# The last steps before the experts: weights 44 and 45 fetched ahead, unread products on TensorE, and a softmax step moved on VectorE

## The chip, the cores and the metric

The kernel runs on one core of one Trainium2 chip. Its time is the device time of one execution in microseconds (us). [...]

## The reference

Attention with a memory term, and after it a soft mixture of experts over the attention's output:

```python
scores = scale * np.matmul(q, k.transpose(0, 1, 3, 2))          # 8 batches, 8 heads, 576 rows, 64 wide, causal
a = softmax(scores); local = a @ v
mem_out = (phi(q) @ M_prev) / (phi(q) @ z_prev)                 # phi = elu + 1
x = g * mem_out + (1 - g) * local                               # reshaped to 4608 x 512
logits = x @ phi                                                # 32 slots
d = softmax of logits over the 4608 rows
slot_input = d.T @ x                                            # 8 experts, 4 slots each
slot_out[e] = relu(slot_input[e] @ w1[e]) @ w2[e]               # w1 512x1024, w2 1024x512
c = softmax of logits over the 32 slots
out = c @ slot_out                                              # 4608 x 512
```

All data are 32-bit floats. The softmax over the 4608 rows must be complete before the first expert can start, so attention and experts can't overlap.

## The kernel before

**Two halves.** The list `SEQ` writes the attention out by hand, 32 head pairs, with the logits and the running softmax over rows between them. Each word is an operation, the head pair or row group it works on (`y` for the one-off steps at the end), and after a colon the PSUM slot that it takes (0 to 3, two banks each). Every engine takes its instructions in the order in which the words emit them; the function `pin` fixes it. Behind the list come the experts, written as plain calls: `f1` (first layer, four of them), `f2` (second layer), `g1` and `g2` (sum over experts), and 18 times `comb`, which makes one block of the output (512 KB) and stores it.

**Weights.** They are 64 blocks of 512 KB. Block x goes where `WORD[x]` says: an empty word is a tile of its own, a name is a buffer of the attention that is no longer used (`FREE`). The words `w@0` to `w@43` fetch 44 blocks during the attention. The other 20 are fetched by the loop over `reload` behind `f1(1,1)` in the program, into the tiles of blocks 0 to 19, each as soon as its `f1` has read the old block. All these transfers and all stores are issued by SyncE (SP) in order. `STAGE` names the block tiles in which `comb` puts its results.

**The chain between the halves.** For the last head pair `mu@31` (VectorE, L485) scales the attention, `ad.0@31` adds its two parts into `x` (L502; the table `EV` says on which engine). `x3.3@7` transposes them on TensorE (L429), `x3e.3` copies them out (ScalarE), `x1.3` multiplies with phi (L610), `y4` takes the running minimum (VectorE, L620). `y6`, `y6m`, `y8` and `y8n` bring the minimum over all slots to `ngm`; `y5` makes the exponentials, `y7` and `y7e` transpose them; `y9.0` and `y9.1` (L742) sum the last rows of x with them into one PSUM tile, `y9a.0` and `y9a.1` (L747) add that tile's halves to `acc`; `y8e` makes `es` (L734); `y10` (L756) gives the experts' input, `y10e` copies it out, and `f1(0,0)` (L847) can start. `y11` and `y12` (L766) are for the denominator.

**The other softmax.** `z1` transposes the logits of eight row groups (TensorE, L429) into PSUM slot 0, and `z2` takes from them, in four VectorE instructions (L786, L787), the minimum over each row's slots. `c0` reads the result, behind `f1(0,0)` on ScalarE.

The last words of the list, with the chain in them, and how a product's tile is taken:

```python
ad.1@31 m.0@31 w@40:+ x1.0@7:2 dn.0@31 x1.1@7 x1.2@7 mu.0@31 w@36:+ ad.0@31 x3.3@7:0 w@41:+ x3e.3@7 x1.3@7 y4@y w@42:+
y6@y:2 y5@y z1@y:0 y6m@y y7@y:3 y8@y w@43:+ z2@y y7e@y y9.0@y:3 y9.1@y y8n@y y9a.0@y y8a@y y9a.1@y y8e@y y11@y y10@y:3
y12@y y10e@y y12e@y
```

Of the kernel before, what the change touches and what calls it, by code (L numbers as in the profile page):

```python
# [176 lines left out]
mx.2.0@31 m.1@30 ex.2.1@31 yz@y t.A@31:1 dn.1@30 ex.2.0@31 w@34:+ x3.1@7:2 mu.1@30 ex.0.1@31 t.B@31:3 te.AX@31  # L177
te.AY@31 ad.1@30 x3e.1@7 av.1@30:0 te.BX@31 w@35:+ te.BY@31 av.0@30 ex.1.0@31 m.0@30 t.C@31:3 dn.0@30 w@37:+ mu.0@30
av.2@31:2 te.CY@31 te.CX@31 ad.0@30 av.3@31 w@38:+ m.1@31 x3.2@7:3 w@39:+ dn.1@31 av.1@31:0 mu.1@31 x3e.2@7 av.0@31
ad.1@31 m.0@31 w@40:+ x1.0@7:2 dn.0@31 x1.1@7 x1.2@7 mu.0@31 w@36:+ ad.0@31 x3.3@7:0 w@41:+ x3e.3@7 x1.3@7 y4@y w@42:+  # L180
y6@y:2 y5@y z1@y:0 y6m@y y7@y:3 y8@y w@43:+ z2@y y7e@y y9.0@y:3 y9.1@y y8n@y y9a.0@y y8a@y y9a.1@y y8e@y y11@y y10@y:3
y12@y y10e@y y12e@y
""".split()

EV = {o: e for e, x in dict(
    a="""
# [17 lines left out]
    p="""  # L204
# [21 lines left out]
        ate@10 te.CY@16 te.CX@16 x2a@3 te.AY@19 te.BX@19 ate@12 te.CY@20 x3e.0@5 te.AY@22 te.CY@22 x3e.2@5 te.CX@23  # L226
        te.AY@25 x3e.0@8 te.BX@25 te.CX@25 te.AY@26 te.BX@26 x3e.1@6 te.CY@26 te.CX@27 te.BX@29 te.BX@30 te.CX@30
        te.AY@31 te.BX@31
    """,
).items() for o in x.split()}  # L230

GO = [0, 1, 2, 3, 4, 5, 8, 6, 7]
WORD = ['', '', '', '', '', '', '', '', '', '', '', '', '', '', '', '', '', '', '', '', '', '', 'xa0', 'xa1', 'au', 'qk0', 'K', 'X', 'p3', 'p2', 'p1', 'qk1', 'x0', 'x1', 'K', 'X', 'xd0', 'p3', 'p2', 'p1', 'at0', 'at1', 'vm', 'xd1']
WARM = 6
STAGE = [20, 21, 22, 23, 24, 25, 26, 27, 28, 29, 30, 31, 32, 33, 34, 35, 36, 37]


@with_exitstack
def tile_attn_soft_moe(ctx, tc, qk, vm, au, beta, phi, w1, w2, cst, out):
    nc = tc.nc  # L240
# [3 lines left out]
    cs = const.tile([128, 256], F32, name="cs")  # L244
    ident = cs[:, 0:128]
# [446 lines left out]
    def op_w(x):  # L692
        wload(x, *(FREE[WORD[x]] if WORD[x] else (wres, f"w{x}", None)))

    y = {}

    def op_y4(_):
        slot_max(cT[:, 8], xs[GO[8]]["p1"][:, 0:128], mrun[0], mrun[1])  # L700
# [141 lines left out]

    def f1(eg, f):
        ps = pf()
        for c in range(4):
            for g in range(4):
                nc.tensor.matmul(ps[32 * g:32 * g + 32, :], si[:, c, 32 * (4 * eg + g):32 * (4 * eg + g) + 32],  # L847
                                 wt[0, eg, f, c // 2, g][:, c % 2, :], start=c == 0, stop=c == 3)
        h = hs[eg, f] = dbl.tile([128, 512], F32, name="f")
        nc.scalar.activation(h, ps, AF.Relu)  # L850

# [63 lines left out]
    def comb(dh, g):  # L915
# [110 lines left out]
```

## Time and profile before

| | us |
|---|---|
| median of 3 runs | 412.38 |
| lowest and highest run | 409.0 and 412.43 |
| the profiled execution | 411.43 |
| its span, first to last instruction | 409.7 |
| attention, up to the last head pair's sums | to about 337 |
| chain between the halves | 337.4 to 347.5 |
| experts, until the last block is computed | 347.5 to 398 |
| last stores, nothing else running | 398 to 408 |

Times below are microseconds from the start of the span. 1.7 us of the execution lie outside the span.

### The profile page before, as it was taken

What the parts mean: (1) busy time and instruction counts of PE and PEld (TensorE: products, weight loads), DVE (VectorE), ACT (ScalarE), POOL (GpSimd) and SP (SyncE); (2) the same over time, 40 slices, a digit from 0 to 9 for tenths busy, and PEclk for the clock granted to TensorE, in tenths of its full rate; (3) what the DMA queues carried; (4) which work ended last, traced back from release to release, by engine and by line L of the source; (5) the groups of instructions that cost most, each with busy time, mean ns of one, the idle gap of its engine ahead of it and who ended that gap; (6) DMA issues with size and microseconds to landing.
All of it is one profiled execution on the core that took longest, in us unless ns stands there. A gap on an engine that the chain in (4) does not pass through costs nothing.

```text
span 409.7 us, 19301 instructions
## 1 busy us (share of the span) xinstructions
PE 371.6 (91%) x8115; PEld 301.3 (74%) x8115; DVE 303.2 (74%) x1136; ACT 295.6 (72%) x741; POOL 198.0 (48%) x255
## 2 busy tenths in 40 slices
PE   7799999989899999999989999999999977999970
PEld 3688987878788878888979788888897864244350
DVE  2879888889888898889888798888988645232560
ACT  1778998788889788989878779877898721211560
POOL 0647765477648637666657476654765310000000
PEclk9889999999999999999999999999999996899995
DMA  8425554745556564666656533434537985599998
GB/s 280 128 83 156 180 173 146 243 133 192 162 164 190 188 211 120 195 193 182 179 150 195 159 102 97 126 117 137 197 102 223 341 301 203 230 407 390 333 334 261
DMA packets 35542, 80.97 MB, mean 198 GB/s; under 512 B 3328, under 2 KB 12800, under 8 KB 35456
## 3 DMA queue, kind: packets, MB, share of 16 engines
q1 hardware_dynamic: 35168, 79.66, 60.3%
q8 instruction: 64, 1.05, 1.1%
q14 instruction: 22, 0.18, 0.2%
q10 hardware_dynamic: 288, 0.08, 0.1%
HBM read 70.29 MB, written 9.44 MB: 195 GB/s over the span
## 4 chain that ended last, share of the span: by engine, by line
PE 49%; ACT 24%; DVE 16%; issue 4%; DMA 3%; SPq 1%; POOLq 0%; POOL 0%; DVEq 0%; ACTq 0%
ACT p L426 13%; PE psD L461 11%; PE psD L429 9%; PE psD L393 9%; DVE p L420 7%; ACT at L290 6%; PE pf L847 4%; PE pf L864 4%; PE psD L471 4%; DVE at L293 3%; DMA qk<-in_qk_dram 2%; ACT xd L290 2%; PE pa L921 2%; DVE w L485 1%; PE psD L654 1%
## 5 line engine op out<-in xcount | busy, mean ns | idle before, releaser
L426 ACT ACTIVATE p<-p,nm 128x576 f32<-128x576 f32 (+3 forms) x256 | 144.1, 608 | 12.4 <-DVE nm L420 11.9
L420 DVE CUSTOM_DVE_ANT_0 p<-psD,mk 128x448 f32<-128x448 f32 (+3 forms) x256 | 127.4, 536 | 9.3 <-PE psD L393 7.0
L461 PE MATMUL psD<-vm,at 128*64 128x65 f32 x2560 | 89.8, 224 | 4.7 <-DVE at L293 2.0
L393 PE MATMUL psD<-K,X 64*128 64x320 f32 (+3 forms) x768 | 91.8, 355 | 2.0 <-DVE at L293 0.5
L290 ACT COPY at<-psD 128x512 f32<-128x512 f32 (+1 forms) x153 | 77.7, 551 | 20.3 <-PE psD L429 17.8
L461 PEld LDWEIGHTS psD<-vm,at 128*64 128x64 f32 x2560 | 80.8, 138 | 14.0 <-issue 3.2
L429 PE MATMUL psD<-cs,p 64*128 64x64 f32 x1408 | 65.4, 227 | 7.4 <-ACT p L426 4.4
L393 PEld LDWEIGHTS psD<-K,X 64*128 64x128 f32 x768 | 63.5, 188 | 8.4 <-DVE at L293 1.0
L429 PEld LDWEIGHTS psD<-cs,p 64*128 64x128 f32 x1408 | 57.6, 140 | 13.1 <-ACT p L426 6.6
L502 POOL TENSOR_TENSOR x<-w 128x256 f32<-128x256 f32 x64 | 46.9, 734 | 36.1 <-DVE w L485 35.1
L485 DVE TENSOR_TENSOR w<-psD,R 128x512 f32<-128x512 f32 x64 | 44.2, 690 | 3.5
L372 POOL TENSOR_TENSOR K<-qk,K 128x576 fp32r<-128x576 f32 x30 | 42.6, 1421 | 2.2
L364 POOL TENSOR_TENSOR X<-qk,X 128x512 fp32r<-128x512 f32 x31 | 39.8, 1284 | 0.7
L376 POOL TENSOR_SCALAR f<-qk 128x512 f32<-128x512 f32 x32 | 19.9, 621 | 35.4 <-PE psD L471 29.8
L471 PE MATMUL psD<-vm,f 64*64 64x65 f32 x1024 | 36.8, 233 | 0.0
L293 DVE COPY at<-psD 128x384 f32<-128x384 f32 (+1 forms) x39 | 23.9, 621 | 15.8 <-ACT at L290 15.2
L295 POOL TENSOR_SCALAR K<-qk 128x576 fp32r<-128x576 f32 x30 | 20.2, 673 | 29.4 <-PE psD L393 24.0
L473 PE MATMUL psD<-vm,at 64*64 64x65 f32 x512 | 33.5, 218 | 0.0
L471 PEld LDWEIGHTS psD<-vm,f 64*64 64x64 f32 x1024 | 28.2, 132 | 5.7 <-issue 1.7
L420 DVE DVE_READ_ACCUMULATOR2_ANT nm<- 128x1 f32 x320 | 26.6, 83 | 0.0
L473 PEld LDWEIGHTS psD<-vm,at 64*64 64x64 f32 x512 | 26.4, 135 | 0.0
L290 ACT COPY xd<-psD 128x512 f32<-128x512 f32 x32 | 18.3, 575 | 9.2 <-PE psD L429 9.0
(186 smaller groups left out, 525.8 us busy)
## 6 DMA issues: line engine op xcount, KB each, us to landing
w<-in_w_dram SPq DMA_DIRECT2D x42, 512.0 KB, 5.1
vm<-in_vm_dram SPq DMA_DIRECT2D x32, 422.5 KB, 3.9
qk<-in_qk_dram SPq DMA_DIRECT2D x32, 288.0 KB, 3.0
qk<-in_qk_dram SPq DMA_DIRECT2D x32, 256.0 KB, 3.5
au<-in_au_dram SPq DMA_DIRECT2D x16, 258.0 KB, 3.2
p<-in_w_dram SPq DMA_DIRECT2D x6, 512.0 KB, 5.1
xa<-in_w_dram SPq DMA_DIRECT2D x2, 512.0 KB, 4.7
x<-in_w_dram SPq DMA_DIRECT2D x2, 512.0 KB, 4.6
```

Source lines behind the costliest of these rows:

```text
L290: nc.scalar.copy(o, i)
L364: ALU_ENG[ev("qlo", n)].tensor_tensor(out=x[:, 1], in0=st[n]["q"], in1=x[:, 0].bitcast(F32), op=ALU.subtract)
L372: ALU_ENG[ev("klo", n)].tensor_tensor(out=x[:, 1], in0=st[n]["k"], in1=x[:, 0].bitcast(F32), op=ALU.subtract)
L393: nc.tensor.matmul(ps[:, h, c:c + k1 - k0], s["X"][ROW[h], x, 128 * i:128 * i + 128], s["K"][ROW[h], y, o + k0:o + k1], start=(x, y) == (0 ...
L420: nc.vector.tensor_tensor_reduce(out=s["p", i][:, h, k0:k1], in0=s["s", u][:, h, c:c + k1 - k0], in1=maskq[:, o + k0:o + k1], op0=ALU.add, ...
L426: nc.scalar.activation(p, p, AF.Exp, scale=-1.0, bias=s["nm"][:, 2 * i + h:2 * i + h + 1])
L429: nc.tensor.transpose(out=o, in_=i, identity=ident[ROW[r], ROW[r]])
L461: nc.tensor.matmul(s["u", u][64 * c:64 * c + 64, h, 65 * x + 130:65 * x + 195], at_block(i, 2 * k + h)[:, c], s["v"][:, k, h], start=first ...
L471: nc.tensor.matmul(s["u", u][64 * c:64 * c + 64, h, 65 * x:65 * x + 65], s["f"][ROW[h], o:o + 64], s["m"][ROW[h]], start=False, stop=x == ...
L473: nc.tensor.matmul(s["u", u][64:128, h, 65 * x + 130:65 * x + 195], atq[i][ROW[h]], s["vr"][ROW[h], i], start=False, stop=x == 1)
L485: nc.vector.tensor_tensor(out=w, in0=s["u", u][:, :, 0:260].rearrange("a h (x d) -> a h x d", d=65)[:, :, :, 0:64], in1=s["R", u].rearrang ...
L502: ALU_ENG[ev(f"ad.{u}", n)].tensor_tensor(out=o, in0=w[:, :, 0:2], in1=w[:, :, 2:4], op=ALU.add)
```

## The change

Six edits, all in the chain between the halves or in the transfers around it.

- `ad.0@31` is on VectorE (it was on GpSimd).
- `z2` stands behind `y10e` on VectorE (it stood ahead of `y8n`), and `z1` takes PSUM slot 1 (it was 0).
- `y9.1` stands behind `y9a.0`, and `y9a.1` behind `y8e`.
- `y12` stands ahead of `y10e` (as it did on TensorE), and a new operation `fill.n` multiplies the identity with n columns of a constant on TensorE; nothing reads its result. Two of 256 columns stand ahead of `x3.3`, one of 256 behind it, one of 128 ahead of `y6`, one of 256 ahead of `y10`, one of 128 ahead of `f1(0,0)`.
- `w@44` and `w@45` follow `w@43` in the list. Block 44 has a tile of its own; block 45 lies in two pieces in the buffers `at` and `vm` and is fetched by two transfers of 256 KB. The loop over `reload` then has 18 blocks.
- `STAGE` starts at block 18 (it was 20).

```diff
-y6@y:2 y5@y z1@y:0 y6m@y y7@y:3 y8@y w@43:+ z2@y y7e@y y9.0@y:3 y9.1@y y8n@y y9a.0@y y8a@y y9a.1@y y8e@y y11@y y10@y:3
+fill.256@y w@41:+ x3e.3@7 x1.3@7 w@42:+ w@43:+ fill.128@y y4@y y6@y:2 y5@y z1@y:1 y6m@y y7@y:3 y8@y w@44 w@45 y7e@y
...
     def wload(x, pool, name, half=None):
         l, *i, g = order[x]
+        if isinstance(name, tuple):
+            for c in range(2):
+                nc.sync.dma_start(out=name[c], in_=(w1[4 * i[0] + g, i[1], i[2]] if l == 0 else w2[4 * i[1] + g, i[0], i[2]]).rearrange("a (c x) y -> a c (x y)", c=2)[:, c])
+            wt[order[x]] = [p.rearrange("a (c x) -> a c x", c=1 + l) for p in name]
+            wslot[order[x]] = (pool, name, half)
+            return
...
+    def op_fill(n):
+
+        if slots:
+            y["fill"] = bank()[:, 0]
+        nc.tensor.matmul(y["fill"][:, 0:int(n)], ident, cs[:, 0:int(n)], start=True, stop=True)
```

How the instructions stand, engine by engine. TensorE, from the last transpose of x to the transposes of `z1`, before (L610 is `x1`, L429 on `x` is `x3.3`, L707 is `y6`, L429 on `cT` is `z1`):

```order
L429 MATMUL psD_7763<-cs,x 128x64 [waits PE_49,Pool_49]
L429 MATMUL psD_7763<-cs,x 128x64 x7
L610 MATMUL psD_7744<-xd,ph 32x128 [waits Activation_49]
L610 MATMUL psD_7744<-xd,ph 32x128 x3
L707 MATMUL psD_7780<-cs,mrun_65 1x128 [waits DVE_49]
L429 MATMUL psD_7787<-cs,cT 128x64 x16
```

The same stretch of the changed kernel (L710 is `fill`, L720 is `y6`):

```order
L710 MATMUL psD_7760<-cs 128x256 x2
L429 MATMUL psD_7766<-cs,x 128x64 [waits DVE_49,PE_49]
L429 MATMUL psD_7766<-cs,x 128x64 x3
L429 MATMUL psD_7766<-cs,x 128x64 [waits Pool_49]
L429 MATMUL psD_7766<-cs,x 128x64 x3
L710 MATMUL psD_7760<-cs 128x256
L610 MATMUL psD_7744<-xd,ph 32x128 [waits Activation_49]
L610 MATMUL psD_7744<-xd,ph 32x128 x3
L710 MATMUL psD_7760<-cs 128x128
L720 MATMUL psD_7786<-cs,mrun_65 1x128 [waits DVE_49]
L429 MATMUL psD_7793<-cs,cT 128x64 [waits PE_49]
```

The transposes now wait for VectorE too, and unread products stand in three places between them.

TensorE from `y8` to the first expert product, before (L724 is `y8`, L742 `y9`, L756 `y10`, L766 `y12`, L847 `f1`):

```order
L724 MATMUL psD_7780<-one,mt 128x1 [waits DVE_49]
L742 MATMUL psD_7819<-x,ext 32x256 [waits Activation_49]
L742 MATMUL psD_7819<-x,ext 32x256 x7
L756 MATMUL psD_7836<-es,acc 128x32 [waits DVE_49,PE_49]
L756 MATMUL psD_7836<-es,acc 128x32 x3
L766 MATMUL psD_7780<-den,cs 128x1 [waits DVE_49]
L847 MATMUL pf_7853<-w_578,mk 32x512 [waits DVE_49]
```

The same stretch of the changed kernel (L737 is `y8`, L755 `y9`, L769 `y10`, L779 `y12`, L860 `f1`):

```order
L737 MATMUL psD_7786<-one,mt 128x1 [waits DVE_49]
L755 MATMUL psD_7823<-x,ext 32x256 [waits Activation_49]
L755 MATMUL psD_7823<-x,ext 32x256 x3
L755 MATMUL psD_7823<-x,ext 32x256 [waits DVE_49]
L755 MATMUL psD_7823<-x,ext 32x256 x3
L710 MATMUL psD_7838<-cs 128x256
L769 MATMUL psD_7842<-es,acc 128x32 [waits DVE_49]
L769 MATMUL psD_7842<-es,acc 128x32 x3
L779 MATMUL psD_7786<-den,cs 128x1 [waits DVE_49]
L710 MATMUL psD_7838<-cs 128x128
L860 MATMUL pf_7865<-w_578,mk 32x512 [waits DVE_49,PE_49]
```

The second half of `y9` now has a wait for VectorE of its own, and an unread product stands ahead of `y10` and of `f1`.

VectorE from `mu.0@31` to the copy `y10e`, before (L786 and L787 are `z2`, L293 on `ngm` is `y8n`, L747 `y9a`, L734 `y8e`, L293 on `mk` is `y10e`):

```order
L485 TENSOR_TENSOR w<-psD_7715,R 128x512
L620 ISA cT,mrun_65<-psD_7744,mk,mrun_64 128x128
...
L786 TENSOR_REDUCE m_7812<-psD_7787 128x16
L787 TENSOR_TENSOR w<-psD_7787,m_7812 128x8x64
L786 TENSOR_REDUCE m_7812<-psD_7787 128x16
L787 TENSOR_TENSOR w<-psD_7787,m_7812 128x8x64
L293 COPY ngm<-psD_7780 128x1
L747 SCALAR_TENSOR_TENSOR acc<-acc,al,psD_7819 128x256 x2
L734 TENSOR_SCALAR es<-cs,ag 128x32
...
L293 COPY mk<-psD_7836 128x32x4
```

The same stretch of the changed kernel (L502 is `ad.0`, L760 `y9a`, L747 `y8e`, L799 and L800 `z2`):

```order
L485 TENSOR_TENSOR w<-psD_7715,R 128x512
L502 TENSOR_TENSOR x<-w 128x2x2x64
L620 ISA cT,mrun_65<-psD_7744,mk,mrun_64 128x128
...
L293 COPY ngm<-psD_7786 128x1
L760 SCALAR_TENSOR_TENSOR acc<-acc,al,psD_7823 128x256
L747 TENSOR_SCALAR es<-cs,ag 128x32
L760 SCALAR_TENSOR_TENSOR acc<-acc,al,psD_7823 128x256
...
L293 COPY mk<-psD_7842 128x32x4
L799 TENSOR_REDUCE m_7850<-psD_7793 128x16
L800 TENSOR_TENSOR w<-psD_7793,m_7850 128x8x64
```

`ad.0` came in, and the four instructions of `z2` went from ahead of `ngm` to behind the copy.

## Rows read from the trace of the kernel before

**Rows 1.** Stretches: length; busy us (instructions) of PE, PEld, DVE, ACT, POOL; PEclk, DMA share, GB/s.

```profile
343.60:352.40 8.80, 7.28 (x46) 3.47 (x46) 2.50 (x10) 0.29 (x1) 0.00 (x0) 0.57 0.05 8
...
352.40:378.60 26.20, 25.55 (x350) 10.99 (x342) 7.44 (x14) 5.95 (x12) 0.00 (x0) 1.00 1.00 397
...
378.60:379.00 0.40, 0.40 (x11) 0.24 (x8) 0.40 (x1) 0.40 (x2) 0.00 (x0) 1.00 0.63 182
...
379.00:407.80 28.80, 17.11 (x210) 9.48 (x206) 11.50 (x18) 13.02 (x34) 0.00 (x0) 0.85 1.00 328
```

**Rows 2.** Timeline of SP: start, length of the run of issues, line, transfer, count.

```profile
351.16 19.35 SPq L683 DMA_DIRECT2D w<-in_w_dram  x20
...
377.90 1.60 SPq L931 DMA_DIRECT2D out_dram<-w  x2
...
389.09 1.02 SPq L931 DMA_DIRECT2D out_dram<-X  x1
...
392.13 1.30 SPq L931 DMA_DIRECT2D out_dram<-p  x2
```

**Rows 3.** The chain that ended last, first-layer products: start, us, engine, tile, line, count.

```profile
347.51 8.91 PE pf L847 x64
...
356.87 3.61 PE pf L847 x32
```

**Rows 4.** Stretches of four us, columns as in Rows 1.

```profile
13.00:17.00 4.00, 2.44 (x50) 1.94 (x48) 4.00 (x23) 2.50 (x6) 2.12 (x4) 0.97 0.25 74
...
333.00:337.00 4.00, 2.99 (x84) 2.34 (x80) 1.75 (x6) 0.59 (x1) 0.72 (x1) 1.00 0.65 238
...
337.00:341.00 4.00, 1.61 (x33) 1.08 (x35) 1.11 (x5) 1.27 (x4) 0.72 (x1) 1.00 0.75 267
...
341.00:345.00 4.00, 2.72 (x27) 1.25 (x22) 3.71 (x9) 0.56 (x2) 0.00 (x0) 0.50 0.63 257
```

**Rows 5.** Timeline between the halves: start, us, engine, line, instruction, count, idle before.

```profile
336.68 0.69 DVE L485 TENSOR_TENSOR w<-psD,R 128x512 f32<-128x512 f32 x1
...
337.45 0.72 POOL L502 TENSOR_TENSOR x<-w 128x256 f32<-128x256 f32 x1 [2.29 <-DVE w L485]
...
338.23 0.46 PE L429 MATMUL psD<-cs,x 64*128 64x64 f32 x8 [1.31 <-POOL x L502]
...
341.28 0.58 PE L724 MATMUL psD<-one,mt 1*128 1x1 f32 x2
...
341.79 1.94 PE L742 MATMUL psD<-x,ext 128*32 128x256 f32 x16
...
343.40 0.69 DVE L787 TENSOR_TENSOR w<-psD,m 128x512 f32<-128x512 f32 x1
...
344.07 0.86 DVE L747 SCALAR_TENSOR_TENSOR acc<-acc,al,psD 128x256 f32<-128x256 f32 x2
...
345.24 1.89 PE L756 MATMUL psD<-es,acc 128*128 128x32 f32 x8 [1.51 <-DVE es L734]
...
346.94 0.56 PE L766 MATMUL psD<-den,cs 128*128 128x1 f32 x2
...
347.16 0.29 DVE L293 COPY mk<-psD 128x128 f32<-128x128 f32 x1 [1.64 <-PE psD L756]
```

**Rows 6.** VectorE's groups by shape: shapes, count, busy us, mean ns, idle before.

```profile
L578 DVE TENSOR_TENSOR aw<-psD,aR 128x256 f32<-128x256 f32 x16 | 6.7, 421 | 0.4
```

**Rows 7.** Timeline of TensorE in the second layer, two successive products of one column group.

```profile
368.25 0.40 PE L864 MATMUL pf<-xd,x 128*32 128x256 f32 x1
...
368.49 0.38 PE L864 MATMUL pf<-xd,x 128*32 128x256 f32 x1
```

**Rows 8.** Single lines: least, median and longest ns, first and last start, shapes.

```profile
L756 PEld LDWEIGHTS psD<-es,acc x8: 288/333/338, 345.2 to 346.7; 128*128 128x128 f32 x8
...
L912 PEld LDWEIGHTS pa<-w,cs x4: 186/188/189, 374.2 to 389.5; 128*128 128x128 f32 x4
...
L912 PE MATMUL pa<-w,cs x4: 379/416/483, 374.2 to 389.7; 128*128 128x256 f32 x4
```

More of the change, by code (lines that the diff above doesn't have):

```diff
@@ L179 @@
 av.2@31:2 te.CY@31 te.CX@31 ad.0@30 av.3@31 w@38:+ m.1@31 x3.2@7:3 w@39:+ dn.1@31 av.1@31:0 mu.1@31 x3e.2@7 av.0@31
-ad.1@31 m.0@31 w@40:+ x1.0@7:2 dn.0@31 x1.1@7 x1.2@7 mu.0@31 w@36:+ ad.0@31 x3.3@7:0 w@41:+ x3e.3@7 x1.3@7 y4@y w@42:+
-y6@y:2 y5@y z1@y:0 y6m@y y7@y:3 y8@y w@43:+ z2@y y7e@y y9.0@y:3 y9.1@y y8n@y y9a.0@y y8a@y y9a.1@y y8e@y y11@y y10@y:3
-y12@y y10e@y y12e@y
+ad.1@31 m.0@31 w@40:+ x1.0@7:2 dn.0@31 x1.1@7 x1.2@7 fill.256@y:1 fill.256@y mu.0@31 w@36:+ ad.0@31 x3.3@7:0
+fill.256@y w@41:+ x3e.3@7 x1.3@7 w@42:+ w@43:+ fill.128@y y4@y y6@y:2 y5@y z1@y:1 y6m@y y7@y:3 y8@y w@44 w@45 y7e@y
+y9.0@y:3 y8n@y y8a@y y9a.0@y y9.1@y y8e@y y9a.1@y fill.256@y:0 y11@y y10@y:3 y12@y fill.128@y y10e@y z2@y y12e@y
 """.split()
@@ L220 @@
         ad.0@27 ad.1@28 qp1@30 ad.0@28 qhi@31 qlo@31 khi@31 klo@31 ad.1@29 qp1@31 ad.0@29 ad.1@30 ad.0@30 ad.1@31
-        ad.0@31
     """,
@@ L228 @@
         te.AY@31 te.BX@31
+        ad.0@31
     """,
@@ L232 @@
 GO = [0, 1, 2, 3, 4, 5, 8, 6, 7]
-WORD = ['', '', '', '', '', '', '', '', '', '', '', '', '', '', '', '', '', '', '', '', '', '', 'xa0', 'xa1', 'au', 'qk0', 'K', 'X', 'p3', 'p2', 'p1', 'qk1', 'x0', 'x1', 'K', 'X', 'xd0', 'p3', 'p2', 'p1', 'at0', 'at1', 'vm', 'xd1']
+WORD = ['', '', '', '', '', '', '', '', '', '', '', '', '', '', '', '', '', '', '', '', '', '', 'xa0', 'xa1', 'au', 'qk0', 'K', 'X', 'p3', 'p2', 'p1', 'qk1', 'x0', 'x1', 'K', 'X', 'xd0', 'p3', 'p2', 'p1', 'at0', 'at1', 'vm', 'xd1', '', 's0']
 WARM = 6
-STAGE = [20, 21, 22, 23, 24, 25, 26, 27, 28, 29, 30, 31, 32, 33, 34, 35, 36, 37]
+STAGE = [18, 19, 20, 21, 22, 23, 24, 25, 26, 27, 28, 29, 30, 31, 32, 33, 34, 35]
 @with_exitstack
@@ L679, in wload @@
             t = t.rearrange("a (c x) -> a c x", c=2)
+            wt[order[x]] = [t[:, 0:1], t[:, 1:2]]
             nc.sync.dma_start(out=t, in_=w1[4 * i[0] + g, i[1], i[2]])
@@ L682, in wload @@
             t = t.rearrange("a (c x) -> a c x", c=4)
+            wt[order[x]] = [t[:, 0:2], t[:, 2:4]]
             nc.sync.dma_start(out=t, in_=w2[4 * i[1] + g, i[0], i[2]])
-        wt[order[x]] = t
         wslot[order[x]] = (pool, name, half)
-    FREE = {"xa0": (spl, "xa", 0), "xa1": (spl, "xa", 1), "X": (dbl, "X", None), "K": (dbl, "K", None),
+    FREE = {"s0": (None, (ats[:, 2048:2560], vmf[:, 1024:1536]), None), "xa0": (spl, "xa", 0), "xa1": (spl, "xa", 1), "X": (dbl, "X", None), "K": (dbl, "K", None),
             "qk0": (None, qkf[:, 0:1024], None), "qk1": (None, qkf[:, QK:QK + 1024], None), "vm": (None, vmf[:, 0:1024], None), "p3": (dbl, "p3", None), "p2": (dbl, "p2", None), "p1": (dbl, "p1", None),
@@ L847, in f1 @@
                 nc.tensor.matmul(ps[32 * g:32 * g + 32, :], si[:, c, 32 * (4 * eg + g):32 * (4 * eg + g) + 32],
-                                 wt[0, eg, f, c // 2, g][:, c % 2, :], start=c == 0, stop=c == 3)
+                                 wt[0, eg, f, c // 2, g][c % 2][:, 0, :], start=c == 0, stop=c == 3)
         h = hs[eg, f] = dbl.tile([128, 512], F32, name="f")
@@ L863, in f2 @@
             for g in range(4):
-                nc.tensor.matmul(po[dh][32 * g:32 * g + 32, 0:256], hT[:, eg, 4 * f + c, 32 * g:32 * g + 32], wt[1, dh, eg, f, g][:, c, :],
+                nc.tensor.matmul(po[dh][32 * g:32 * g + 32, 0:256], hT[:, eg, 4 * f + c, 32 * g:32 * g + 32], wt[1, dh, eg, f, g][c // 2][:, c % 2, :],
                                  start=(eg, f, c) == (0, 0, 0), stop=(eg, f, c) == (1, 1, 3))
```

## The prediction

> **What bounds the kernel now.** I read the tail backwards, since all that is changed lies in it. The stretches [rows 1] come first: from 379.0 to 407.8 the DMA engines are full (share 1.00, 328 GB/s) with stores, from 352.4 to 378.6 full with weights (397 GB/s), and before that, from 343.6 to 352.4, nearly empty (0.05). So the end is the first store's start plus 28.8 us. What sets that start? SP's timeline [rows 2] issues the first store at 377.90, and its bytes flow at 379.0, some 1.1 us later; the last weights end at 378.6. Between them is a dip of 0.4 us at share 0.63 [rows 1]: the weights were over when the stores began. The start is therefore set by TensorE, which made the first block, and the chain [rows 3] shows TensorE's first-layer products back to 347.51 without a wait for a weight. So: end = start of `f1(0,0)`, plus the work from there to the first store, plus 28.8.
>
> Two things stand out on that path. First, the clock. It is 0.50 from 341 on [rows 4], and the two first `f1` take 8.91 us, where the third takes 3.61 [rows 3]. Second, the chain itself [rows 5]: GpSimd's add of 0.72 us, `z2` on VectorE until 344.09, ahead of the steps that `y10` waits for, and `y9` and `y10` at 1.94 and 1.89 us under the low clock.
>
> The later stretch needs one check, that it moves as a whole. The last store of the first nine is issued at 389.09 and the tenth at 392.13 [rows 2]. Nine stores at 28.8 / 18 = 1.6 us keep the DMA engines busy until 379.0 + 14.4 = 393.4, and the tenth's bytes come 1.1 after its issue, at 393.2. That closes with 0.2 us to spare; since TensorE's work from the first store to the tenth is unchanged, it closes after the change as well.
>
> **The change part by part**, on the clock of the profiled execution.
>
> `ad.0` on VectorE. Before, `mu` ends at 337.37, GpSimd adds from 337.45 to 338.17, and TensorE starts at 338.23 [rows 5]. VectorE has no such add in the trace. Its nearest row, 256 elements from PSUM, is 421 ns [rows 6]; half of the 512-element `mu` is 0.35, and GpSimd's own 0.72 is the upper bound. I take 0.42, the same size: end 337.82, TensorE at 337.88, a gain of 0.35 (0.05 to 0.42). Nothing waits behind it on VectorE, whose next step is `y4`.
>
> The fills ahead of `y9`. One product of 256 columns at full clock takes 416 ns, two are issued for a fill, and the products overlap: the second-layer pair in rows 7 starts 0.24 apart. So two fills hold TensorE some 4 x 0.24 = 0.96 us, from about 336.9, which is just the pause until 337.88; the later ones (0.48, 0.24) lie beside ScalarE's copy `x3e` and beside `y4`. Nought on the path, at most 0.2 if the two start late; if the clock is low while they run, they cost double (below).
>
> `y8` took 0.58 us under the low clock and ended at 341.86 [rows 5], beyond the copy that `y9` waits for, and `y9` follows its loads. At full clock that is over: gain 0.1 (0 to 0.2).
>
> `y9` to `y10`: 341.79 to 345.24, 3.45 us. With `z2` gone from VectorE, what is late next is a chain that this change makes serial: the second half of `y9` has a wait for VectorE in the built order, and the only VectorE step on its PSUM tile by then is `y9a.0`, which reads the first half. So it goes half, add, half, add. A half at full clock is two products, 0.24 + 0.40 = 0.64 [rows 7]; an add is half of 0.86, with its own start, 0.47 [rows 5]; handoffs are 0.05 each. Sum 2 x 0.64 + 2 x 0.47 + 4 x 0.05 = 2.4, so `y10` starts 1.0 us earlier. If the halves weren't serial, it would be 0.5 us better. `y8e` fits between the adds. The fill ahead of `y10` (0.48) fits under the second add.
>
> `y10` to `f1`: 345.24 to 347.51, 2.27 us. `y10` is a row of loads of 128 columns; such a load is 333 ns under the low clock and 188 under the full one [rows 8], so 1.89 becomes 1.07, a gain of 0.8. In front of `f1` there are now `y12` and a fill of 128: 0.28 (half of 0.56 [rows 5]) and 0.24, against the copy `y10e` of 0.29 plus handoffs, so 0.1 is lost (0 to 0.4). Net 0.7.
>
> `z2` behind `y10e`. Its four instructions of 0.69 us run beside `f1(0,0)`, 2.8 us against 3.6 for an `f1` [rows 3]; ScalarE wants the result only after that `f1`'s own output. With slot 1, no first-layer product waits for `z2`'s reads. If it were 1 us longer, `c0` would slip, and nothing on the path before the combine. Nought.
>
> First layer: 8.91 against 2 x 3.61 less one overlap of some 0.2, so 7.0: gain 1.9 (1.7 to 1.9).
>
> Blocks 44 and 45. At 397 GB/s the two are 1.05 MB / 0.397 = 2.6 us of DMA time, moved from the full stretch to the empty one [rows 1]. SP issues them behind `w@43`, all three before the first reload at 351.16 [rows 2], which itself waits for `f1`; nothing else is queued behind them. But the weights already ended before the stores, and `f1`, which starts them, moves as the first store does. So the loads end 2.6 us earlier into a gap that the stores can't use. Nought, from no gain up to 0.4 (the dip). `STAGE` moves with the reloads: nought.
>
> Sum: 0.35 + 0.1 + 1.0 + 0.7 + 1.9 = 4.05 us, all on the path, so the profiled 411.43 would be 407.4. The median of the runs shown is 0.95 above the profiled execution. If that lies in how late the low clock ends, a held clock takes it away; if elsewhere, it stays. I take half: **407.8 us**.
>
> **Will the clock hold?** Nearly 3 us of the 4 rest on that. The clock was at its low level from 341 on, after four us in which TensorE was busy for 1.61; it fell within 13 to 17 (PEclk 0.97 there), in which TensorE was busy for 2.44; and it was 1.00 over 333 to 337, with 2.99 [rows 4]. The fills bring 337 to 341 to 1.61 + 0.96 + 0.48 + 0.24 = 3.3 us. The four after that hold `y8`, `y9`, one fill and `y10`, by the terms above 0.3 + 1.28 + 0.48 + 1.07 = 3.1. Both are more like the stretch in which it held than like those before a fall. That is likeness, no more: busy time counts loads and transposes as it counts products, and after 341 TensorE was busy for 2.72 of four us and the clock stayed low [rows 4].
>
> **The rivals.** (1) The clock falls again before `f1`, because what TensorE does in this chain is for the most part not products: of the 33 instructions counted from 337 to 341 [rows 4], 24 are transposes (8 of `x3.3` in rows 5, 16 of `z1`), and `y10` loads 128 columns to multiply 32. Against it stand the fills, which are products in every place. Say it falls as `y10` starts: of the sum, 0.35, 0.1 and 1.0 stay, the fill and `y12` in front of `f1` cost double (0.3 lost), and the first two `f1` keep their 8.91. That gives 411.43 - 1.15 = 410.3; with the fall earlier or the rise later, 409 to 411.5. [...] (2) The end on the other side: TensorE's clock is low already when the two fills run, as it would be if it fell a few us earlier than in the profiled execution. Then each fill costs double, 1.9 us from 336.9 in a pause of 0.96, which puts `x3.3` 0.9 late; the later fills add 0.3 + 0.4 + 0.5; the moves give back 0.35 + 1.0; and a rise that comes later still leaves the second half of the first two `f1` low, 1.7. Together +2.4: 413.8. It decides from the point at which the clock is low at 337; the rows from 333 to 337 (1.00) speak against it. (3) More than forecast: the halves of `y9` aren't serial, and all of the 0.95 goes: 411.43 - 4.55 = 406.9, or less. (4) The load-ahead counts, because stores were held by the last weights: the dip of 0.4 allows 0.4 at most, 407.4. It lies inside the forecast.
>
> **How the numbers follow.** The forecast with (4) and its bounds, 406.4 to 408.9, has 0.58; (3) has 0.08; (1) has 0.29; (2) and worse have 0.05. The range must take in part of (1): low 406.0, high 410.6. One per cent, about what a measurement of this kernel can tell from no change, is 4.1 us, so the border lies at 408.3, close above the forecast: about three quarters of the forecast's 0.58 lie below it, with (3) that makes 0.52 for faster; 0.44 for within 1%, mostly (1); 0.04 for slower.
>
> **What would show it.** In the changed kernel's profile: PEclk 1.00 from 337 to the end of the first layer; `x3.3` about 0.35 earlier; the halves of `y9` 1.2 us apart with an add between; `f1(0,0)` near 345.4 and the two first `f1` in about 7.0 us; the first reload near 347.4; the weights over some 3 us before the first store, a hole in the DMA share there; the stores again 28.8 us without a hole. What would make it wrong: a stretch of 0.50 after 341 (then rival 1), stores that take longer or have a hole between the ninth and the tenth, or a `f1` that waits for a weight.

## The result, and the profile after

| | before | after |
|---|---|---|
| median of 20 runs, us | 412.09 | 408.03 |
| lowest and highest | 409.0, 414.12 | 405.42, 411.83 |
| profiled execution, its span | 411.43, 409.7 | 409.12, 407.3 |

The ratio of after to before is 0.9901, 95% interval 0.9877 to 0.9926: faster by 1.0%. Medians are over all runs; the ratios leave out slow runs, those more than 1.5% above the fastest of their kernel, and so need not be quotients of the medians. The forecast was 407.8, the range 406.0 to 410.6.

The two profiled executions stand only 2.3 us apart. To compare them, one must know that the sum after begins later: `mu` starts at 337.66 where it started at 336.68 [rows 5], though nothing that it waits for was changed (the last section comes back to this). So each reading below is counted from `mu`'s end (338.35 after, 337.37 before).

The stretches of after, with the columns of [rows 1]; first the way ahead of the first reload, then weights, a hole, and stores:

```profile
344.40:348.50 4.10, 4.04 (x34) 2.22 (x38) 3.19 (x8) 0.00 (x0) 0.00 (x0) 1.00 0.74 285
348.50:373.30 24.80, 24.15 (x326) 10.35 (x318) 7.26 (x15) 4.75 (x9) 0.00 (x0) 1.00 0.97 379
373.30:376.10 2.80, 2.80 (x44) 1.09 (x37) 1.22 (x2) 1.47 (x4) 0.00 (x0) 1.00 0.10 36
376.10:405.20 29.10, 17.23 (x210) 9.62 (x210) 11.62 (x18) 13.12 (x34) 0.00 (x0) 0.86 0.99 324
```

The weights are over 2.8 us before the first store's bytes; the DMA engines stand nearly empty there (0.10), and the stores then take 29.1 us instead of 28.8. SP's timeline gives the issues that answer to [rows 2]; the first row is block 44:

```profile
341.00 0.42 SPq L691 DMA_DIRECT2D w<-in_w_dram  x1
...
348.50 16.80 SPq L691 DMA_DIRECT2D w<-in_w_dram  x18
375.12 4.48 SPq L944 DMA_DIRECT2D out_dram<-w  x4
```

TensorE's granted clock (the column PEclk, a share of the full clock) is 1.00 or 0.50 in the traces before and after, and between the two only where a stretch holds both. In stretches of four us as in [rows 4] it is 1.00 where it had been 0.50 from 341 on. The first row, from the start of the kernel, is used further below:

```profile
12.00:16.00 4.00, 3.83 (x26) 3.25 (x24) 3.60 (x15) 0.76 (x4) 0.62 (x1) 0.50 0.01 5
334.00:338.00 4.00, 3.53 (x105) 2.92 (x103) 1.77 (x6) 0.58 (x1) 0.73 (x1) 1.00 0.79 292
338.00:342.00 4.00, 3.89 (x44) 2.42 (x44) 1.66 (x6) 1.26 (x4) 0.00 (x0) 1.00 0.85 277
342.00:346.00 4.00, 3.27 (x30) 1.92 (x30) 1.67 (x6) 0.56 (x2) 0.00 (x0) 1.00 1.01 383
```

The chain that ended last, first-layer products, answers to [rows 3]: 7.07 us for the first 64 where it had been 8.91.

```profile
346.57 7.07 PE pf L860 x64
354.10 3.62 PE pf L860 x32
```

And the timeline between the halves, to be held against [rows 5]:

```profile
337.66 0.69 DVE L485 TENSOR_TENSOR w<-psD,R 128x512 f32<-128x512 f32 x1
...
337.84 1.13 PE L710 MATMUL psD<-cs 128*128 128x256 f32 x4
...
338.39 0.42 DVE L502 TENSOR_TENSOR x<-w 128x256 f32<-128x256 f32 x1
...
338.96 0.47 PE L429 MATMUL psD<-cs,x 64*128 64x64 f32 x8
...
342.34 0.64 PE L755 MATMUL psD<-x,ext 128*32 128x256 f32 x8
...
343.13 0.48 DVE L760 SCALAR_TENSOR_TENSOR acc<-acc,al,psD 128x256 f32<-128x256 f32 x1 [0.63 <-PE psD L755]
...
343.66 0.64 PE L755 MATMUL psD<-x,ext 128*32 128x256 f32 x8 [0.68 <-DVE acc L760]
...
344.37 0.48 DVE L760 SCALAR_TENSOR_TENSOR acc<-acc,al,psD 128x256 f32<-128x256 f32 x1 [0.61 <-PE psD L755]
...
344.91 1.08 PE L769 MATMUL psD<-es,acc 128*128 128x32 f32 x8
...
346.04 0.47 PE L710 MATMUL psD<-cs 128*128 128x128 f32 x2
...
346.23 0.68 DVE L799 TENSOR_REDUCE m<-psD 128x16 f32<-128x512 f32 x1
```

L710 is a fill; `z2` (L799) now runs beside `f1`. The halves of `y9` are 1.32 us apart with an add between them, where 1.2 was forecast.

### The profile page after: what moved, and what is told of

Its sections match the earlier page's. It is cut to its first block, busy times and chain, and to the rows that moved or that the text cites. A ratio compares the mean times of both kernels' runs of the same rounds, so it can differ in the third digit from the quotient of the medians.

```text
span 407.3 us, 19323 instructions
## 1 busy us (share of the span) xinstructions
PE 371.9 (91%) x8127; PEld 302.8 (74%) x8127; DVE 304.0 (75%) x1137; ACT 295.0 (72%) x741; POOL 197.2 (48%) x254
## 4 chain that ended last, share of the span: by engine, by line
PE 51%; ACT 25%; DVE 15%; issue 3%; DMA 2%; SPq 1%; DVEq 0%; ACTq 0%
ACT p L426 13%; PE psD L461 11%; PE psD L393 10%; PE psD L429 9%; DVE p L420 6%; ACT at L290 6%; PE pf L877 4%; PE psD L471 4%; PE pf L860 4%; DVE at L293 3%; DMA qk<-in_qk_dram 2%; ACT xd L290 2%; PE pa L934 2%; PE psD L654 1%; DVE w L485 1%
## 5 line engine op out<-in xcount | busy, mean ns | idle before, releaser
L393 PE MATMUL psD<-K,X 64*128 64x320 f32 (+3 forms) x768 | 93.8, 362 | 1.7 <-DVE at L293 0.5
L429 PE MATMUL psD<-cs,p 64*128 64x64 f32 x1408 | 65.6, 228 | 7.1 <-ACT p L426 3.9
L393 PEld LDWEIGHTS psD<-K,X 64*128 64x128 f32 x768 | 65.0, 193 | 8.3 <-DVE at L293 1.0
L429 PEld LDWEIGHTS psD<-cs,p 64*128 64x128 f32 x1408 | 57.7, 140 | 13.1 <-ACT p L426 6.2
L502 POOL TENSOR_TENSOR x<-w 128x256 f32<-128x256 f32 x63 | 46.2, 734 | 33.8 <-DVE w L485 32.8
L293 DVE COPY at<-psD 128x384 f32<-128x384 f32 (+1 forms) x39 | 23.9, 621 | 15.8 <-ACT at L290 15.1
```

The source lines that it names most:

```text
L393: nc.tensor.matmul(ps[:, h, c:c + k1 - k0], s["X"][ROW[h], x, 128 * i:128 * i + 128], s["K"][ROW[h], y, o + k0:o + k1], start=(x, y) == (0 ...
L429: nc.tensor.transpose(out=o, in_=i, identity=ident[ROW[r], ROW[r]])
L502: ALU_ENG[ev(f"ad.{u}", n)].tensor_tensor(out=o, in0=w[:, :, 0:2], in1=w[:, :, 2:4], op=ALU.add)
```

## The experiments

The theory to be tested: the gain is TensorE's alone. The fills hold the clock at 1.00 and the moves shorten the chain; the two weights loaded ahead bring nothing. Its rivals: the load-ahead carries the gain; the moves alone hold the clock; or transposes would not do as fills.

One table for all kernels. The pieces are read from each profiled execution: from `mu`'s end to `f1(0,0)`, from there to the third `f1`, and from the first store's issue to the end. Between the last two, from the third `f1` to the first store's issue, every kernel takes 21.02 or 21.03. The column "high clock" counts the runs whose mean granted clock was 0.975 or more. None of the 81 runs of the kernel before that were made beside these reached that (at most 0.974), so I count a run that did as one that kept the clock between the halves. That is an inference, since only one run of each kernel has a trace. Below 0.975 either can be: the mean also counts the low clock at the start (3.4 to 13.7 us in the profiles, last section) and under the last stores (7.6 to 11.5 us). The last column is good to about 0.1.

| kernel | median us | ratio to before, 95% | high clock | mu to f1 | two f1 | stores |
|---|---|---|---|---|---|---|
| before | 411.2 to 412.1 | | 0 of 81 | 10.14 | 9.36 | 31.8 |
| after | 408.03 | 0.9901 (0.9877 to 0.9926) | 15 of 20 | 8.22 | 7.53 | 32.2 |
| no fills | 410.76 | 0.9993 (0.9963 to 1.0023) | 0 of 12 | 10.31 | 8.83 | 31.9 |
| fills alone | 408.5 | 0.9927 (0.9893 to 0.9961) | 7 of 12 | 9.33 | 7.53 | 31.5 |
| not ahead | 407.22 | 0.9913 (0.9883 to 0.9944) | 8 of 12 | 8.21 | 7.53 | 31.6 |
| ahead alone | 411.5 | 1.0007 (0.9977 to 1.0036) | 0 of 12 | 10.59 | 10.31 | 31.6 |
| z2 early | 414.02 | 1.0057 (1.0023 to 1.009) | 0 of 12 | 11.78 | 10.05 | 31.5 |
| ad.0 on GpSimd | 407.02 | 0.9908 (0.9871 to 0.9945) | 7 of 10 | 8.47 | 7.53 | 32.4 |
| transposes, 8 | 408.91 | 0.9921 (0.9885 to 0.9956) | 6 of 12 | 9.00 | 9.87 | 31.8 |
| transposes, 12 | 407.96 | 0.9905 (0.9866 to 0.9945) | 4 of 8 | 8.41 | 8.84 | 31.8 |
| two tiles | 405.7 | 0.9873 (0.9834 to 0.9912) | 4 of 6 | 7.48 | 7.54 | 31.8 |
| two tiles, again | 406.01 | 0.9887 (0.9848 to 0.9925) | 6 of 6 | 7.49 | 7.53 | 32.3 |
| two tiles, warm | 405.79 | 0.9876 (0.9835 to 0.9916) | 6 of 6 | 7.48 | 7.53 | 32.3 |
| two tiles, lean | 407.69 | 0.9892 (0.9855 to 0.9929) | 4 of 12 | 7.27 | 7.53 | 31.4 |

**No fills.** Every `fill` word is taken out of the changed kernel's order.

```diff
-x1.2@7 fill.256@y:1 fill.256@y mu.0@31 ...
+x1.2@7 mu.0@31 ...
```

> The changed kernel without its fill products; the moves of z2, ad.0 and the two more weights stay. Theory A (the fills hold TensorE's clock, and the moves work by themselves): the granted clock falls to 0.50 somewhere between 339 and 343 as it did before, the first 64 first-layer products take 8.9 us again, and the way from the end of mu to f1 is about 9 to 9.5 us (8.22 with the fills, 10.14 before). The time is 2.5 to 3.3 us above the changed kernel, about 411, 0 to 1.5 below the kernel before. Rival M (the denser chain of the moved steps holds the clock by itself, and the fills are ornament): clock 1.00, f1 7.1, time as the changed kernel, 408, or 0.2 less since no fill stands ahead of f1.

The gain is gone within the noise: 410.76, and not one run at a high clock. The stretch in which the clock is low (from 339.8 to 350.1), then the timeline and the chain:

```profile
339.80:350.90 11.10, 9.81 (x71) 5.09 (x74) 5.28 (x15) 1.14 (x5) 0.00 (x0) 0.54 0.56 224
```

```profile
341.63 1.08 PE L755 MATMUL psD<-x,ext 128*32 128x256 f32 x8
...
343.39 1.08 PE L755 MATMUL psD<-x,ext 128*32 128x256 f32 x8 [0.68 <-DVE acc L760]
...
345.08 1.92 PE L769 MATMUL psD<-es,acc 128*128 128x32 f32 x8 [0.60 <-DVE acc L760]
```

```profile
347.38 8.38 PE pf L860 x64
```

The moves alone are worth nothing, less than I had expected (10.31 against 9 to 9.5). From `y9` to `y10` it is 3.45 us, exactly as before [rows 5]: what `z2` gave back, the halves lost again by being serial, at 1.08 each under the low clock. The clock also fell sooner, 2.7 us after `mu`'s end where it had been 3.6 (341.0).

**Fills alone.** The kernel before, with the fills at the same places.

```diff
-y8e@y y11@y y10@y:3 y12@y y10e@y ...
+y8e@y fill.256@y y11@y y10@y:3 y12@y fill.128@y y10e@y ...
```

> The kernel before with the same fills at the same places and nothing moved. Theory A with its weak point: the pause of 2.4 us in which z2 holds VectorE ahead of y9a stays, so the clock has less to hold it there. If it holds, the way from mu's end to f1 is about 9 us (10.14 less 0.1 for y8 and about 0.9 for y10), the first 64 first-layer products 7.1, and the time is 2.5 to 3 below the kernel before, 409.3. If it falls in that pause, f1 is 8.9 and the time is 0 to 1 below, or up to 0.5 above, because the fills in front of y10 and f1 cost double. I hold the fall for a little likelier (0.55). Rival B (the two weights loaded ahead carry the gain): no gain either way, 412.

About three quarters of the gain: 408.5. In the profile the clock held at 1.00, through this pause of 1.87 us, which both halves of `y9` and a fill precede:

```profile
344.25 0.70 PE L703 MATMUL psD<-cs 128*128 128x256 f32 x2
...
345.66 0.86 DVE L753 SCALAR_TENSOR_TENSOR acc<-acc,al,psD 128x256 f32<-128x256 f32 x2
...
346.82 1.05 PE L762 MATMUL psD<-es,acc 128*128 128x32 f32 x8 [1.87 <-DVE es L740]
```

I had thought the fall a little likelier; in the profile it didn't come, and in at least 7 of 12 runs it didn't either.

**Not ahead, and ahead alone.** The two more blocks are taken from the changed kernel, and given alone to the kernel before.

```diff
-y8@y w@44 w@45 y7e@y
+y8@y y7e@y
-WORD = [..., 'xd1', '', 's0']
+WORD = [..., 'xd1']
-STAGE = [18, 19, 20, ..., 35]
+STAGE = [20, ..., 35, 36, 37]
```

> The changed kernel with 44 weight blocks ahead, as before, and the last two back among the reloads. Theory A: TensorE's path is untouched, the weights end 2.6 us later, at the first store or a few tenths after it; the hole of about 2.8 us in the DMA share ahead of the first store is gone, and the first store's bytes begin 0 to 0.4 later. Time within 0.4 of the changed kernel (408.0 to 408.4). Rival B (the end follows the sum of the DMA bytes): +2.6, 410.6.

> The kernel before with blocks 44 and 45 loaded ahead and nothing else of the change. Theory A: TensorE's way is that of before, the clock falls as before, and the two more blocks leave a hole in the DMA share ahead of the first store; time 412 as before, or 0.2 to 0.4 more, since the kernel without the load-ahead had its stores done some 0.3 sooner after the first was issued. Rival B: 2.6 us of DMA time is taken from the end, 409.2.

Without them 407.22, no slower than with; with them alone 411.5 against 411.24, no gain. This excludes the rival of 2.6 us from both sides. A small price is possible, and not shown. In the profile without the blocks the stores follow the last weights, and after the dip between them their share is full (the first two rows, in steps of one us from 371); in that of the changed kernel they start after a hole, at 0.85 and 0.94 (from 376):

```profile
371.00:372.00 1.00, 1.00 (x19) 0.39 (x16) 0.65 (x1) 0.75 (x2) 0.00 (x0) 1.00 0.63 246
372.00:373.00 1.00, 1.00 (x20) 0.49 (x20) 0.44 (x2) 0.59 (x3) 0.00 (x0) 1.00 1.00 343
```

```profile
376.00:377.00 1.00, 1.00 (x20) 0.58 (x20) 0.44 (x2) 0.59 (x2) 0.00 (x0) 1.00 0.85 303
377.00:378.00 1.00, 1.00 (x24) 0.45 (x13) 0.51 (x1) 0.56 (x2) 0.00 (x0) 1.00 0.94 312
```

But "two tiles" (below) has the blocks and the hole too, and its first us of stores is full:

```profile
374.60:375.60 1.00, 1.00 (x20) 0.50 (x24) 0.44 (x2) 0.59 (x3) 0.00 (x0) 1.00 0.99 341
```

So the hole by itself does not make a slow start. From the store's issue to the end, the ten profiles with the blocks take 31.5 to 32.4, 31.95 in the mean; the four without 31.4 to 31.8, 31.6. The ranges overlap, and what makes the difference of the means stays open. In "ahead alone" the clock fell as it does before, a little earlier and for longer (0.50 from 339.8 to 353.5), so that profile says nothing on the path.

**z2 early.** `z2` stands again ahead of the adds on VectorE, all else as changed.

```diff
-y8@y w@44 w@45 y7e@y ... y10e@y z2@y y12e@y
+y8@y z2@y w@44 w@45 y7e@y ... y10e@y y12e@y
```

> The changed kernel with z2 back ahead of y9a on VectorE, its PSUM slot kept. Theory: z2's 2.8 us begin at the same place as y8's end, y9a waits for them, y10 starts 1.5 to 1.8 us later, and the same comes out at f1 and in the time (409.7). In the kernel with the fills alone the same pause let the clock stand in most executions, so I expect 1.00 in the first layer here too; if it falls, f1 is 8.9 and the time 411.5. Rival: the move of z2 was worth nothing by itself, since ScalarE's copy and the adds bound y10: y10 within 0.3, time as the changed kernel.

414.02, 6.0 above the changed kernel and slower than before. I had put down 1.7 and a clock that holds; 1.7 is only where it begins.

```profile
343.69 0.64 PE L755 MATMUL psD<-x,ext 128*32 128x256 f32 x8
...
346.11 0.47 DVE L760 SCALAR_TENSOR_TENSOR acc<-acc,al,psD 128x256 f32<-128x256 f32 x1
...
346.63 1.08 PE L755 MATMUL psD<-x,ext 128*32 128x256 f32 x8 [2.30 <-DVE acc L760]
```

```profile
351.48 9.60 PE pf L860 x64
```

The add waits for `z2`, the second half for the add, and the fill stands behind that half; so TensorE has nothing at all for 2.30 us, the clock falls to 0.50 at 346.4, and TensorE's work behind it takes 1.6 to 1.7 times as long (the half 1.08 for 0.64, the fill 1.22 for 0.70, `y10` 1.76 for 1.08). It is 3.56 more up to `f1`, of which the longer pause is 1.62 (2.30 for 0.68), and 2.52 more in the two first `f1`, together 6.1. The three parts of the change thus hang together: fills alone held the clock, the serial halves without fills ate up `z2`'s gain, and fills with serial halves but without `z2`'s move were worse than nothing.

**ad.0 on GpSimd.** The add goes back to its old engine: in the table `EV` its word moves from VectorE's list (the last line of the cut) to GpSimd's.

```diff
-... ad.0@30 ad.1@31
+... ad.0@30 ad.1@31 ad.0@31
...
-        ad.0@31
```

> The changed kernel with ad.0@31 back on GpSimd. Theory: the add takes 0.72 instead of 0.42, so from mu's end to x3.3 it is 0.86 again instead of 0.61, and all behind it 0.25 to 0.3 later; the time 0.3 up, not to be told from the changed kernel's. Rival: the fills in front of x3.3 reach that far anyway (they end 0.07 after the add in the changed kernel), and only 0.2 or less is seen.

8.47 against 8.22 from `mu`'s end to `f1`: 0.25 on the path, as expected, and not to be seen in the time.

**Transposes as fills.** Each fill is 8, or in a second kernel 12, transposes instead of products (half as many for a fill of 128).

```diff
-            y["fill"] = bank()[:, 0]
-        nc.tensor.matmul(y["fill"][:, 0:int(n)], ident, cs[:, 0:int(n)], start=True, stop=True)
+            y["fill"] = bank()
+        for x in range(int(n) // 32):        # second kernel: // 20
+            turn(y["fill"][:, x % 2, 0:64], cs[ROW[x % 2], 0:128], x % 2)
```

> The changed kernel with each fill made of transposes of 64 x 128 instead of products: 8 for a fill of 256 columns, 4 for one of 128, which by the eight of x3.3 (0.47 us) hold TensorE as long as the products did. Theory A (any busy work holds the clock): as the changed kernel, clock 1.00 to the end of the first layer, f1's first 64 in 7.1, 408.0 +- 0.4. [...]

> The changed kernel with fills of transposes as in the run before, but 12 for a fill of 256 columns and 6 for one of 128: eight of them held TensorE some 0.36 us there, against 0.5 for the two products of a fill, so 12 and 6 make up for it. In the run before, the 12 executions fell into two heaps by their mean clock, six at 0.970 to 0.971 near 410 us and six at 0.975 to 0.986 near 406; the profiled one is of the first. Theory A (busy time alone decides, and those fills were too short): now most executions hold the clock as with products, 10 of 12 above 0.973, median 408 or below. Theory C (transposes count for less, whatever their time): still half of the executions or more at 0.971 or below, median 408.5 to 410.

In both profiled executions the clock fell, at 343.4 in the first kernel and at 346.9 in the second (windows from the fall to just behind the rise, at 350.3 in both):

```profile
343.40:350.70 7.30, 7.24 (x41) 3.15 (x44) 3.13 (x8) 0.00 (x0) 0.00 (x0) 0.53 0.31 119
```

```profile
346.90:350.70 3.80, 3.74 (x28) 1.26 (x30) 3.09 (x7) 0.00 (x0) 0.00 (x0) 0.55 0.42 164
```

But 6 of 12 and 4 of 8 runs have a high clock, where without fills none of 12 had. None of these runs has a trace, and a fall as short as the second kernel's (3.4 us, to 350.3) could hide in a mean of 0.979. In the first kernel five are at 0.982 or more, with 405.3 to 406.47 us against 409.4 to 411.6 for the six at 0.970 and 0.971. So transposes do help to hold the clock (10 of 20 runs against 0 of 12). Whether less surely than products stays open: 10 of 20 runs against 15 of 20 is within chance, while in the profiles the clock fell in both of these kernels and held in all eight with products other than "z2 early". The fills of one kernel add up to 2.44, 3.10 and 3.49 us of TensorE (8 transposes, 12, products), so even the second kernel's were shorter than the products. Whether a transpose holds the clock less well than a product of the same length stays open.

**Two tiles.** The second half of `y9` gets its own PSUM tile and follows the first at once; the fill goes into that tile's other bank, ahead of the adds.

```diff
-y9a.0@y y9.1@y y8e@y y9a.1@y fill.256@y:0 y11@y
+y9.1@y:0 fill.256@y:9 y9a.0@y y8e@y y9a.1@y y11@y
...
-        if half == 0:
-            y["pp"] = bank()[:, 0]
+        pp = y["pp", half] = bank()
```

> The changed kernel with the second half of y9 in a PSUM tile of its own, so that it follows the first half without a wait for the add, and the fill behind it, ahead of the adds. The chain half, add, half, add of 2.57 us from y9 to y10 becomes half, then add, add: 0.64 + 0.05 + 0.48 + 0.05 + the copy y8e of 0.13 to 0.2 + 0.48 + 0.1 = 1.9 to 2.0. So y10 and everything behind it 0.5 to 0.6 us earlier (theory: the serial halves cost this). Rival: the adds wait for something else, for instance the scalar from ScalarE (y8a) or y8e, and nothing is gained. The time would fall by 0.5, less than the comparison can tell; the trace decides.

> The kernel with the second half of y9 in its own PSUM tile once more, to have more executions beside the two below and on the same chip. As before: 405.7, about 1 us below the changed kernel at like mean clock.

```profile
341.52 1.07 PE L754 MATMUL psD<-x,ext 128*32 128x256 f32 x16
...
342.31 0.48 DVE L759 SCALAR_TENSOR_TENSOR acc<-acc,al,psD 128x256 f32<-128x256 f32 x1 [0.64 <-PE psD L754]
...
343.09 1.34 PE L768 MATMUL psD<-es,acc 128*128 128x32 f32 x8
...
343.26 0.48 DVE L759 SCALAR_TENSOR_TENSOR acc<-acc,al,psD 128x256 f32<-128x256 f32 x1 [0.32 <-PE psD L710]
```

From `y9` to `y10` it is 1.57 instead of 2.57: `y10` now starts on the first half while the second is added, and gives 0.26 of that back by waiting inside (1.34 for 1.08). The second add is itself held 0.32 by the fill (L710), which stands ahead of it in the same tile. Net 0.74 to `f1`, more than the 0.5 to 0.6 expected, and the medians are 2 us below the changed kernel's, of which the path explains 0.7; with 6 runs each the rest is scatter or a clock kept in more of them (10 of 12).

**Two tiles, warm, and lean.** On top of two tiles, one more warming product; or, in another kernel, no blocks ahead (their edits are those of "not ahead") and no last fill.

```diff
-WARM = 6
+WARM = 7
```

> The kernel with the second half of y9 in its own PSUM tile, and one more warming product at the start (7 for 6). Theory S (the scatter between executions of one kernel comes from a low clock between 11 and 25 us, which follows the pause of 1 to 2.5 us ahead of the first 64-row products): the extra product shortens that pause by 0.6 to 1.1 us, fewer executions fall there, and the median is 0.3 to 1 below the one without it, 405; the mean clocks lie more closely around 0.98. Rival: the fall there comes from the pauses after 14 us, and nothing changes, or the extra product only delays the first 64-row products, 0 to +0.6.

```diff
-y12@y fill.128@y y10e@y
+y12@y y10e@y
```

> The kernel with the second half of y9 in its own PSUM tile, without the two weights ahead and without the last fill (the one between y12 and f1). Theory A: the load-ahead is worth nothing and the last fill stands 0.2 us in front of f1, so the time is 0 to 0.5 below the one with both, 405.4; the clock holds as before. Rival: without the last fill the clock falls in the first layer in some executions, which would show as mean clocks of 0.971 or below and times near 410.

The warming product raises the mean clock (0.980 to 0.985 in its six runs, 0.973 to 0.981 in the twelve without it), and does nothing to the time. From 8 to 24 us, first without it, then with it:

```profile
8.00:16.00 8.00, 5.59 (x48) 4.06 (x46) 4.69 (x16) 2.76 (x9) 1.50 (x2) 0.79 0.52 187
16.00:24.00 8.00, 6.21 (x78) 5.46 (x76) 5.53 (x25) 7.25 (x20) 6.56 (x8) 0.66 0.33 97
```

```profile
8.00:16.00 8.00, 6.18 (x69) 3.65 (x67) 5.96 (x29) 4.45 (x12) 2.55 (x5) 1.00 0.56 209
16.00:24.00 8.00, 7.33 (x102) 6.90 (x102) 5.57 (x22) 7.02 (x19) 5.53 (x6) 0.57 0.35 102
```

All six of those means are at 0.980 or above (without it one of 12), but the median is 405.79 against 405.7 and 406.01. The low clock at the start isn't gone in its profile: it lasts 6.8 us, from 16.2, where the two profiles without the product have 10.2 and 6.8 us. The lean kernel has the shortest path (7.27, the last fill's 0.2), but only 4 of 12 runs at a high clock and 407.69. Whether it lost the clock for want of that fill or by the start can't be told; in its profile the clock held between the halves, and `mu` ended at 340.86, 2.5 us later than in the changed kernel (last section). The lowest medians are those of two tiles, with or without the warming product: 405.7 to 406.0, about 1.2% below before. Against the changed kernel itself their intervals still overlap.

## Why the prediction was right

Counted from `mu`'s end, the changed kernel reaches the first store 36.77 us later, before it was 40.53: 3.76 less, where the sum had 4.05.

- **`ad.0`**: 0.42 as taken; `x3.3` starts 0.61 after `mu`'s end instead of 0.86. Gain 0.25 for 0.35: the two fills ahead of it took 1.13 for 0.96 and end 0.15 after the add, within the 0.2 that was allowed for them. Undoing the edit gave the 0.25 back.
- **`y8`**: from the start of `x3.3` to that of `y9` 3.38 for 3.56, a gain of 0.18 for 0.1 (0 to 0.2).
- **`y9` to `y10`**: 2.57 for 3.45, a gain of 0.88 for 1.0. The mechanism, half, add, half, add, is the one in the trace; the first add starts 0.15 behind its half, where 0.05 was reckoned. Two tiles, which take it away, made it 1.57. So the third rival was real as a possibility, and bigger (0.74 net) than its 0.5.
- **`y10` to `f1`**: 1.66 for 2.27, 0.61 for 0.7; the last fill is on the path for 0.2, as the lean kernel shows.
- **First layer**: 7.07 for 8.91, 1.84 for 1.9.
- **Blocks 44 and 45**: the hole ahead of the first store is there, and neither kernel that isolates them shows a gain. I bounded them from nought to a gain of 0.4; what the profiles show is no gain; whether there is a loss of up to 0.4 stays open. The stores were to be again 28.8; they are 29.1, and no run shows why.
- **`z2`**: 346.23 to 349.03, beside `f1`, at no cost, as said. But costing it apart from the serial halves hid what "z2 early" shows: its move is what lets fills and serial halves go together.
- **The clock** is where the argument was thinnest, a likeness of busy times (which, read from the column PE, hold products and transposes; loads have a column of their own). Without fills it fell in the profiled execution, and none of 12 runs has a high clock, so the likeness pointed the right way. Rival 1 didn't come about in the profiled execution, nor in the 15 runs with a high clock; in the other four (0.966 to 0.974, 409.16 to 411.83 us) it can't be excluded. Its reason, that TensorE's work here is for the most part not products, has the runs of "transposes, 8" against it: with transposes for fills six of 12 means lie at 0.975 to 0.986, without fills none of 12 lies above 0.971. Its number was fair: the six of "transposes, 8" whose mean clock was 0.971 or less lie at 409.4 to 411.6, against its 409 to 411.5. Rival 2, the end on the other side, at 413.8, was reached by no run of the changed kernel (at most 411.83); "z2 early" ended there by another way, 414.02. That fills cost double under the low clock, as both rivals have it, no run shows: in "z2 early" the two behind the fall took 1.22 and 0.78 us where at 1.00 they take 0.70 and 0.47. Likewise `y12`, put at half of its 0.56, takes 0.36 at 1.00.
- **From profile to median**: I added half of 0.95, for the case that the scatter lies in how late the low clock ends. That case holds in part: from `mu`'s end to the third `f1`, "ahead alone" took 20.90 us where before took 19.50, with the same work on TensorE. But the median of after lies 1.1 below its profiled execution, and much of the scatter arises ahead of `mu` (last section). By the profiled ways the change is worth 72.33 - 68.95 = 3.4 from `mu`'s end to the last, since the sum was 0.3 too large and the stores cost 0.4 that it had not; the medians differ by 4.1. The 0.7 between the two lies within the interval of the ratio (3.0 to 5.1 us), so that 407.8 came so near 408.03 is in part luck. The measured 0.99% lies at the border of one per cent that the forecast drew, so on which side of it a measurement falls is chance.

## What to carry to other kernels

The clock that fell in the sparse chain here (0.50 from 341.0) also slowed the work behind it: of the 3.76 us gained 1.84 lay in the first layer (7.07 for 8.91). So count what runs until the clock rises again. Before loading more ahead, see what ends last at the point the load is to free; here it was compute, and the load only made a hole of 2.8 us. And when two steps share a PSUM tile, read the waits of the built order: here an interleaving that looked harmless turned two overlapping pairs into a chain of four (2.57 us from `y9` to `y10`, with two tiles 1.57).

## What the runs showed that I had not expected

Much of the scatter of some 2 us in the runs of one kernel is there before the change begins, as far as the profiles show. In the 14 profiled executions `mu` ends between 334.1 and 340.9, though nothing ahead of it differs but the first fills and the one warming product. Much of it goes with a low clock at the start: one stretch of 3.4 us, from about 17.5, in the earliest (not ahead); 13.7 us, from 11.3 to 25.0, in the changed kernel (the row of 12 to 16 above, at 0.50). At the first `mu` of the kernel the two are already 3.15 us apart, and lean is beside the changed kernel (in this order: not ahead, changed, lean):

```profile
24.44 0.69 DVE L485 TENSOR_TENSOR w<-psD,R 128x512 f32<-128x512 f32 x1
```

```profile
27.59 0.69 DVE L485 TENSOR_TENSOR w<-psD,R 128x512 f32<-128x512 f32 x1
```

```profile
27.45 0.69 DVE L485 TENSOR_TENSOR w<-psD,R 128x512 f32<-128x512 f32 x1
```

Lean, the latest of all, has 13.7 us too, and the clock fell in it once more, in the middle of the attention, as in no other profile:

```profile
212.80:216.20 3.40, 3.00 (x56) 2.92 (x56) 3.27 (x15) 3.40 (x9) 3.11 (x4) 0.50 0.30 83
```

At the next `mu` it is 1.95 us behind the changed kernel; the rest of its 2.5 us comes in the last head pair and stays open. In the 14 profiles the low clock at the start lasts 3.4 to 13.7 us, and it begins 11 to 17.5 us in, not with the first products (at 1.45 before and after).

The second: by its mean clocks, one and the same program can keep the clock in one run and lose it in the next, as the kernel with 8 transposes seems to, with times in two heaps, 405.3 to 408.5 (0.975 to 0.986) and 409.4 to 411.6 (0.970 and 0.971). Nor do a kernel's runs all follow its profile: with the fills alone the clock held in the profile (a mean of 0.974), and two other runs have means of 0.963 and 0.967, as low as runs of the kernel before.
